# New instruction lists, loads and PSUM banks for an attention block, and a last batch that ends in two parts

## The chip, the cores and the metric

The kernel runs on one core of one Trainium2 chip. The metric is the device time of one execution in microseconds (us), lower is better; the number compared is the median of several executions. The profile is one execution taken by the hardware profiler: it shows when each instruction ran on each engine. The engines are PE (TensorE: matrix multiplications into PSUM), ACT (ScalarE), DVE (VectorE), POOL (GpSimd) and SP (SyncE, which here only issues transfers); PEld is PE's weight load, which overlaps the multiplications. Each engine has its own instruction list and runs it in order; they meet through semaphores.

## The reference

```python
B, Sq, D = 8, 112, 640
H, Sk, Dh = 32, 512, 192
...
q = (lambda x, *d: x.transpose(*d))((x @ wq).reshape(B, Sq, H, Dh), 0, 2, 1, 3)
scores = jnp.einsum("bhqd,bhkd->bhqk", q, k_cache) * (Dh ** -0.5)
p = _softmax(scores, axis=-1)
o = jnp.einsum("bhqk,bhkd->bhqd", p, v_cache)
return (lambda x, *d: x.transpose(*d))(o, 0, 2, 1, 3).reshape(B, Sq, H * Dh) @ wo
```

Inputs and output are bf16. The K and V caches are the bulk of the bytes read: 8 x 32 heads of 512 x 192 each.

## The kernel before

The heads are worked off in four rounds of eight (`NR`, `HU`). A round has the eight batches, and a batch in a round has two steps of four heads (`qd`), so there are 64 steps n (`NN`); n // 2 numbers the K and V blocks. A group g (`NG` = 8) is half a round: four batches, for which the queries and the output product are made together.

What a step needs is made by named operations, and these names stand in the lists:

- `('XT', c)` transposes a piece of x on PE, `evX` copies it out of PSUM.
- `('Q', g, lp, c)` (line 721) is one 128-column piece of the query product for a group: five matmuls of 448 columns; `evQ` copies it out. `('qc', n)` makes a copy shifted by half the partitions, on POOL mostly.
- `('KT', i, p)` (line 673) transposes K on PE for those blocks that were loaded as they lie (`PLAIN`: blocks 0 to 5 and 14; transfer `KN`), 24 transposes of 64 rows each; `evK` copies them out, in two halves. The other blocks come transposed by the transfer itself (`K`, line 158).
- `('Sm', n, j)` and `('St', n, j)` (line 774) are the scores of two heads: `Sm` is the first 128 of the 192 contraction rows, the full array; `St` the remaining 64, two row tiles of 64 side by side.
- `smax`, `exp`, `rc`, `norm` (lines 831, 836, 848, 840) are the softmax: minimum of the negated scores and copy to SBUF on DVE, exponential with its sum on ACT, reciprocal and scaling on DVE.
- `('PT', n)` (line 875) transposes the probabilities: 32 small transposes, row tiles of 64 and 48; `evPT` copies them out, part 0 with 768 and part 1 with 1024 columns. Steps 57 to 61 (`BY_DMA`) are transposed by a transfer instead (`TD`, line 859).
- `('PVt', n)` and `('PVm', n, j)` (lines 907 and 919) are probabilities times values. `PVm` makes 128 of the 192 output rows of each head with the full array, `PVt` (the "value rests") the other 64 of two heads side by side: 16 matmuls with column tiles of 64. `evPV` copies both out.
- `('O', g, m, part)` (line 941) is the output product of a group for one block m of 128 output columns, in two halves of six matmuls; `oacc` adds it to a running sum in `accT` on DVE. For the last group the third batch is done by `O6` (line 974) and the fourth, the last batch of all, by `OL` (line 998); `oacc6` and `oaccL` (lines 1007 and 1011) add these. `OF` (line 1023) transposes a batch of the result back, `oout` copies it to SBUF and the transfer `OUT` (line 646) writes it.

On PE the operations are of three kinds, by how the array is divided: the full array (XT, Q, Sm, PVm, O, O6, OL, OF), rows in two (KT, St, PT) and columns in two (PVt).

Nothing orders itself at run time. `ORDER_PE`, `ORDER_ACT`, `ORDER_DVE`, `ORDER_POOL` and `ORDER_SP` (lines 236 to 574) are written out by hand or by a planner beforehand, and each engine runs its list. `Plan.run` puts a wait ahead of an operation for each semaphore count that its inputs need. `copy` (line 144) takes the engine in whose list a copy stands. `BANKS` (line 575) gives each PSUM tile its bank; a tile waits until the copy of the bank's previous holder is done (`holder`). SP's transfers go out in list order; each waits until its place is free (`k_place_free`, `pv_all`, `q_done`) and, by `AHEAD`, until enough of the earlier ones have landed:

```python
        for i, op in enumerate(ORDER_SP):
            behind = [k for k in range(i) if sum(map(size, ORDER_SP[k + 1:i])) >= AHEAD]
            if behind and op[0] != "OUT":
                P.ops[op]["deps"] = P.ops[op]["deps"] + [ORDER_SP[behind[-1]]]
```

## Time and profile before

| | |
|---|---|
| median of 3 runs | 436.23 us (436.13 to 437.5) |
| the profiled execution's own time | 434.56 us |
| its span, first to last instruction | 432.8 us |
| PE busy | 418.6 us, 97%, 6805 matmuls |
| DVE busy | 345.8 us, 80%, 1087 instructions |
| ACT busy | 335.9 us, 78%, 734 instructions |
| POOL busy | 88.7 us, 20% |
| bytes moved by transfers | 122.05 MB, mean 282 GB/s |

The busy time of an engine is the time in which at least one of its instructions runs. A row of the timeline has the start in us from the beginning of the span, the time until the last of the merged instructions ends, the engine and line, the operation with its output and inputs, the shape (for PE the rows x columns of the array, then the operand), the number of instructions merged, and in brackets the idle time before with what ended it. Matmuls are pipelined, so that the time from one start to the next says what a matmul costs the list, and its own duration does not. A row of the waits has who waited for whom: us in total, times, longest.

### The profile page before, as it was taken

The page shows a single profiled execution, that of the slowest core. Times are in us where ns is not written, and L with a number is a line of the kernel's source. Part 1 is how long each engine was busy: PE and PEld are TensorE (multiplying, and loading weights), DVE is VectorE, ACT ScalarE, POOL GpSimd, SP SyncE. Part 2 cuts the span into 40 slices and gives each one's busy share as a digit, 9 for nine tenths or more (in the row PEclk, how much of TensorE's full clock was granted, in tenths as well). Part 3 has the DMA queues.
Part 4 walks back from the last instruction along what each step waited for, and adds up shares of the span by engine and source line. Part 5 has one row for each costly group of instructions (what it writes and reads, how often), then busy time and mean ns, then how long its engine had stood idle before and what let it go on. Part 6 is the DMA issues. An engine that isn't in the chain of part 4 may idle for free.

```text
span 432.8 us, 16330 instructions
## 1 busy us (share of the span) xinstructions
PE 418.6 (97%) x6805; PEld 289.6 (67%) x6805; DVE 345.8 (80%) x1087; ACT 335.9 (78%) x734; POOL 88.7 (20%) x124
## 2 busy tenths in 40 slices
PE   6999997999999999999999999999999999999996
PEld 4566665666767666677767656776667666666786
DVE  1689878889778888888798897869888688988871
ACT  3489988988868686979877957988778877776774
POOL 0102121222212221322122122212222120212100
PEclk9999999999999999999999999999999999999999
DMA  7999999999999999999999999999999999999872
GB/s 254 371 337 334 335 309 238 326 355 179 229 343 257 220 334 374 341 230 343 290 222 335 299 222 324 368 359 214 244 259 268 211 282 368 312 241 247 207 216 84
DMA packets 218923, 122.05 MB, mean 282 GB/s; under 512 B 165216, under 2 KB 218848, under 8 KB 218848
## 3 DMA queue, kind: packets, MB, share of 16 engines
q1 hardware_dynamic: 218848, 120.99, 107.6%
q8 instruction: 54, 0.88, 0.8%
q14 instruction: 21, 0.17, 0.1%
HBM read 78.22 MB, written 1.15 MB: 183 GB/s over the span
## 4 chain that ended last, share of the span: by engine, by line
PE 86%; DMA 6%; DVE 4%; ACT 1%; issue 1%; SPq 0%; DVEq 0%; ACTq 0%
PE ps L721 19%; PE ps L774 19%; PE ps L941 18%; PE ps L919 12%; PE ps L907 7%; PE ps L875 7%; PE ps L673 2%; DVE s_sb L831 2%; DMA wq_sb<-in_wq_dram 2%; DMA vt<-in_v_cache_dram 2%; DMA wq_sb<-p_sb 1%; DMA accT<-in_k_cache_dram 1%; DVE p_sb L840 1%; PE ps L974 1%; ACT p_sb L836 1%
## 5 line engine op out<-in xcount | busy, mean ns | idle before, releaser
L836 ACT ACTIVATE p_sb<-s_sb,nmx 112x512 bf16<-112x512 f32 x256 | 182.6, 716 | 34.4 <-DVE s_sb L831 28.6
L831 DVE TENSOR_SCALAR_CACHE_REDUCE s_sb<-ps 112x512 f32<-112x512 f32 x256 | 169.5, 683 | 30.1 <-PE ps L774 22.1
L762 POOL COPY qh<-qr 64x672 bf16<-64x672 bf16 x59 | 44.0, 746 | 309.8 <-PE ps L774 266.7
L721 PE MATMUL ps<-xT_sb,wq_sb 128*128 128x448 bf16 x480 | 101.7, 353 | 4.2 <-DMA wq_sb<-in_wq_dram 2.7
L774 PE MATMUL ps<-kt,qr 128*128 128x256 bf16 (+1 forms) x512 | 95.3, 272 | 0.2
L941 PE MATMUL ps<-oT_sb,wo_sb 128*128 128x448 bf16 (+1 forms) x480 | 91.4, 341 | 0.0
L840 DVE TENSOR_SCALAR p_sb<-p_sb,rinv 112x512 bf16<-112x512 bf16 x256 | 88.3, 374 | 0.8
L774 PE MATMUL ps<-kt,qh 128*128 128x256 bf16 (+1 forms) x512 | 87.7, 272 | 0.0
L721 PEld LDWEIGHTS ps<-xT_sb,wq_sb 128*128 128x128 bf16 x480 | 42.6, 98 | 41.0 <-DMA wq_sb<-in_wq_dram 3.7
L941 PEld LDWEIGHTS ps<-oT_sb,wo_sb 128*128 128x128 bf16 x480 | 44.8, 98 | 36.0 <-issue 0.4
L146 ACT ACTIVATE oT_sb<-ps 128x672 bf16<-128x672 f32 x64 | 46.3, 724 | 24.8 <-PE ps L919 24.4
L146 ACT ACTIVATE pT_sb<-ps 128x1024 bf16<-128x1024 bf16 (+1 forms) x61 | 55.8, 921 | 10.9 <-PE ps L875 10.9
L774 PEld LDWEIGHTS ps<-kt,qr 128*128 128x128 bf16 (+1 forms) x512 | 44.1, 96 | 21.4 <-issue 12.9
L919 PE MATMUL ps<-pT_sb,vt 128*128 128x112 bf16 x944 | 55.3, 213 | 0.0
L919 PEld LDWEIGHTS ps<-pT_sb,vt 128*128 128x128 bf16 x944 | 47.5, 98 | 4.0
L836 ACT ACTIVATION_READ_ACCUMULATOR p_sb<-s_sb,nmx 112x1 f32 x256 | 49.1, 192 | 0.0
L774 PEld LDWEIGHTS ps<-kt,qh 128*128 128x128 bf16 (+1 forms) x512 | 44.1, 96 | 6.0
L763 POOL COPY qh<-qr 64x672 bf16<-64x672 bf16 x59 | 44.0, 745 | 2.5
L146 ACT ACTIVATE qr<-ps 128x448 bf16<-128x448 f32 x58 | 31.0, 538 | 14.6 <-PE ps L721 14.4
L147 DVE COPY pT_sb<-ps 128x768 bf16<-128x768 bf16 (+1 forms) x57 | 34.6, 608 | 7.9 <-PE ps L875 7.7
L875 PE MATMUL ps<-ident,p_sb 64*128 64x64 bf16 (+1 forms) x1888 | 37.3, 185 | 1.8 <-issue 1.2
L875 PEld LDWEIGHTS ps<-ident,p_sb 64*128 64x128 bf16 (+1 forms) x1888 | 33.5, 94 | 7.6 <-issue 3.5
(58 smaller groups left out, 268.7 us busy)
## 6 DMA issues: line engine op xcount, KB each, us to landing
vt<-in_v_cache_dram SPq DMA_DIRECT2D x64, 768.0 KB, 6.8
wo_sb<-in_wo_dram SPq DMA_DIRECT2D x8, 960.0 KB, 7.5
wq_sb<-in_wq_dram SPq DMA_DIRECT2D x7, 960.0 KB, 7.3
wo_sb<-in_k_cache_dram SPq DMA_DIRECT2D x6, 768.0 KB, 7.5
accT<-in_k_cache_dram SPq DMA_DIRECT2D x4, 768.0 KB, 6.1
vt<-in_k_cache_dram SPq DMA_DIRECT2D x2, 768.0 KB, 8.5
kt<-in_k_cache_dram SPq DMA_DIRECT2D x2, 768.0 KB, 6.9
out_dram<-xT_sb SPq DMA_DIRECT2D x8, 140.0 KB, 2.3
```

What stands on the lines that cost most here:

```text
L146: return e.activation(dst, src, ACTF.Copy)
L147: return e.tensor_copy(dst, src)
L721: mm = e.matmul(ps[:, bank, 0:SG], w, v, start=(dc == 0), stop=(dc == DC - 1))
L762: e.tensor_copy(dst[64:128, :, 0:3, :], src[0:64])
L763: return e.tensor_copy(dst[0:64, :, 1:4, :], src[64:128])
L774: return e.matmul(ps[:, 2 * j + odd, hs], q, ktb[j][lo:hi, :, blk, h * 128:(h + 1) * 128], start=first, stop=last, skip_group_check=True)
L831: return e.tensor_scalar(s_sb[:, a, :].rearrange("p (e c) -> p e c", e=2), ps[0:SQ, 2 * j:2 * j + 2, h * 256:(h + 1) * 256], -scale, None, ...
L836: return e.activation(p_sb[:, k, :], s_sb[:, a, :], ACTF.Exp, bias=nmx[:, k:k + 1], scale=-1.0, accum_out=rsum[:, k:k + 1])
L840: return e.tensor_scalar(p_sb[:, k, :], p_sb[:, k, :], rinv[:, k:k + 1], None, op0=ALU.mult)
L875: ends.append(e.transpose(psb[:, bank + t, i * w:(i + 1) * w], p_sb[lo:hi, (4 * n + k) % 8, q * 128:(q + 1) * 128], ident[lo:hi, lo:hi]))
L919: mm = e.matmul(ps[:, b0 + j, 2 * h * SQ:(2 * h + 1) * SQ], vtb[:, h0 + 2 * j + h, d0:d0 + 128], pT(j, h, q), start=(q == 0), stop=(q == 3))
L941: mm = e.matmul(ps[:, bank_of["O", g, m], 0:nc_], wo_sb[:, k, m * 128:(m + 1) * 128], oT_sb[:, g % 2, k, 0:nc_], start=(k == 0), stop=(k = ...
```

## The change

All five engine lists but POOL's, the order of loads and the table of banks are replaced. The same operations are done, but for the last batch. What the new lists do differently, as far as it can be said in words:

- PE: neighbours of different kinds number 238 and not 249; in 19 places and not 10 a `PVt` stands directly behind a `PT`. Early on some `KT` and `Q` are exchanged, and `KT` of block 2 comes together.
- ACT and DVE: 10 of the `evK` and 10 of the larger `evPT` copies go from ACT to DVE, 2 `evX` and 1 `evQ` from DVE to ACT.
- SP: V 2 is loaded later and V 0 earlier among the first pieces; later blocks are exchanged; at the end V 31 goes ahead of OUT 2 and OUT 1.
- Banks: other numbers; `XT` 0 and `XT` 1 now share bank 4.

The last batch (7) ends in two parts: `OL` and `oaccL` go by the blocks 0 to 2 and 3 to 4 (`ENDS`, in place of 0, 1, 4 and 2, 3), so that each `oaccL` is one addition; `OF` and `oout` of batch 7 are split in the same way, with a bank each; the transfer waits for both copies. The second copy and that of batch 6 are in DVE's list.

```diff
--- before.py
+++ after.py
         ORDER_PE = [
...
-            ('KT', 0, 0), ('KT', 0, 1), ('Q', 0, 1, 2), ('XT', 4), ('Q', 0, 0, 2), ('Q', 0, 3, 0), ('XT', 5),
-            ('Q', 0, 2, 1), ('Sm', 0, 0), ('Sm', 0, 1), ('St', 0, 0), ('St', 0, 1), ('KT', 0, 3), ('Q', 0, 3, 1),
-            ('Q', 0, 3, 2), ('KT', 0, 2), ('KT', 1, 2), ('KT', 1, 1), ('Q', 0, 2, 0), ('XT', 6), ('Q', 0, 2, 2),
-            ('Q', 1, 0, 1), ('KT', 2, 1), ('KT', 1, 3), ('Sm', 1, 0), ('Sm', 1, 1), ('St', 1, 0), ('St', 1, 1),
-            ('Q', 1, 1, 0), ('KT', 1, 0), ('KT', 2, 3), ('KT', 2, 2), ('Q', 1, 0, 0), ('Q', 1, 0, 2), ('Q', 1, 1, 1),
-            ('Sm', 2, 0), ('Sm', 2, 1), ('KT', 2, 0), ('St', 2, 0), ('St', 2, 1), ('PT', 0), ('Q', 1, 2, 0), ('Q', 1, 3, 2),
...
-            ('Q', 2, 0, 2), ('PT', 5), ('PVt', 4), ('KT', 5, 3), ('PVm', 4, 0), ('PVm', 4, 1), ('Sm', 8, 0), ('Sm', 8, 1),
...
-            ('PVt', 62), ('PVt', 63), ('PVm', 62, 0), ('PVm', 62, 1), ('PVm', 63, 0), ('PVm', 63, 1), ('OF', 5),
-            ('OL', 0, 1), ('OL', 0, 0), ('OL', 1, 0), ('OL', 1, 1), ('OF', 6), ('OF', 7)]
+            ('KT', 0, 0), ('KT', 0, 1), ('Q', 0, 1, 2), ('XT', 4), ('XT', 5), ('Q', 0, 0, 2), ('Q', 0, 3, 0),
+            ('Q', 0, 2, 1), ('Sm', 0, 0), ('Sm', 0, 1), ('KT', 0, 3), ('KT', 0, 2), ('St', 0, 0), ('St', 0, 1),
+            ('Q', 0, 2, 0), ('Q', 0, 3, 2), ('XT', 6), ('Q', 0, 2, 2), ('KT', 1, 1), ('Q', 0, 3, 1), ('Q', 1, 0, 1),
+            ('KT', 1, 2), ('KT', 1, 3), ('KT', 2, 1), ('Sm', 1, 0), ('Sm', 1, 1), ('St', 1, 0), ('St', 1, 1),
+            ('Q', 1, 1, 0), ('Q', 1, 0, 0), ('KT', 1, 0), ('KT', 2, 3), ('KT', 2, 2), ('KT', 2, 0), ('Q', 1, 1, 1),
+            ('Sm', 2, 0), ('Sm', 2, 1), ('St', 2, 0), ('St', 2, 1), ('PT', 0), ('Q', 1, 0, 2), ('Q', 1, 2, 1),
...
+            ('Q', 2, 0, 2), ('Q', 2, 1, 2), ('KT', 5, 3), ('PT', 5), ('PVt', 4), ('PVm', 4, 0), ('PVm', 4, 1),
...
+            ('O', 7, 3, 1), ('PVt', 61), ('PVm', 61, 0), ('PVm', 61, 1), ('O6', 1, 0), ('PT', 62), ('O6', 1, 1), ('OF', 1),
+            ('O6', 0, 0), ('O6', 2, 0), ('OF', 3), ('O6', 0, 1), ('O6', 2, 1), ('PT', 63), ('PVt', 62), ('PVm', 62, 0),
+            ('PVm', 62, 1), ('PVt', 63), ('PVm', 63, 0), ('PVm', 63, 1), ('OL', 0, 0), ('OF', 5), ('OF', 4), ('OL', 1, 0),
+            ('OL', 0, 1), ('OL', 1, 1), ('OF', 6), ('OF', 7, 0), ('OF', 7, 1)]
         ORDER_ACT = [
...
-            ('evPT', 63, 1), ('oout', 4), ('evPV', 62), ('evPV', 63), ('oout', 5), ('oout', 6), ('oout', 7)]
...
+            ('evPT', 62, 1), ('oout', 3), ('evPV', 62), ('evPV', 63), ('oout', 5), ('oout', 4), ('oout', 7, 0)]
         ORDER_DVE = [
...
-            ('norm', 63, 3), ('evPT', 62, 0), ('oacc6', 2), ('evPT', 63, 0), ('oacc6', 1), ('oaccL', 0), ('oaccL', 1)]
...
+            ('norm', 63, 1), ('evPT', 63, 1), ('evPT', 63, 0), ('oacc6', 1), ('oacc6', 0), ('oacc6', 2), ('oaccL', 0),
+            ('oaccL', 1), ('oout', 6), ('oout', 7, 1)]
         ORDER_SP = [
...
-            ('KN', 0, 4, 4), ('KN', 1, 0, 4), ('KN', 1, 4, 4), ('V', 2, 0), ('KN', 2, 0, 4), ('V', 2, 1), ('KN', 2, 4, 4),
-            ('V', 0, 0), ('V', 0, 1), ('KN', 3, 4, 4), ('KN', 4, 4, 4), ('KN', 3, 0, 4), ('KN', 4, 0, 4), ('V', 1, 1),
...
-            ('K', 30), ('K', 31), ('TD', 57), ('TD', 58), ('V', 29, 0), ('V', 29, 1), ('TD', 59), ('TD', 60), ('V', 30, 1),
-            ('V', 30, 0), ('TD', 61), ('OUT', 2), ('OUT', 1), ('V', 31, 0), ('V', 31, 1), ('OUT', 4), ('OUT', 0),
-            ('OUT', 3), ('OUT', 5), ('OUT', 6), ('OUT', 7)]
...
+            ('KN', 0, 4, 4), ('KN', 1, 0, 4), ('KN', 1, 4, 4), ('KN', 2, 0, 4), ('V', 0, 0), ('KN', 2, 4, 4), ('V', 2, 0),
+            ('KN', 3, 4, 4), ('V', 0, 1), ('V', 1, 1), ('KN', 3, 0, 4), ('V', 1, 0), ('KN', 4, 4, 4), ('KN', 4, 0, 4),
...
+            ('K', 30), ('V', 26, 1), ('V', 27, 1), ('V', 26, 0), ('WO', 3, 0), ('V', 27, 0), ('WO', 3, 1), ('V', 28, 0),
+            ('V', 28, 1), ('K', 31), ('TD', 57), ('TD', 58), ('V', 29, 0), ('V', 29, 1), ('TD', 59), ('TD', 60),
+            ('V', 30, 1), ('V', 30, 0), ('TD', 61), ('V', 31, 0), ('OUT', 0), ('V', 31, 1), ('OUT', 2), ('OUT', 1),
+            ('OUT', 5), ('OUT', 3), ('OUT', 4), ('OUT', 6), ('OUT', 7)]
         BANKS = [
...
-            (('XT', 0), 5), (('XT', 1), 4), (('XT', 3), 7), (('XT', 2), 6), (('Q', 0, 1, 1), 7), (('Q', 0, 0, 0), 5),
...
+            (('XT', 0), 4), (('XT', 1), 4), (('XT', 3), 5), (('XT', 2), 6), (('Q', 0, 1, 1), 7), (('Q', 0, 0, 0), 5),
...
+            (('OF', 6), 2), (('OF', 7, 0), 5), (('OF', 7, 1), 0)]
         for kind, *a in ORDER_SP:
...
         for b in range(B):
             def emit(e, b=b):
                 return e.dma_start(out[b], xT_sb[0:SQ, b % DC, 0:D])
-            add("SP", ("OUT", b), [("oout", b)], emit, f"mOUT{b % DC}", 16)
+            add("SP", ("OUT", b), [("oout", b)] if b < B - 1 else [("oout", b, 0), ("oout", b, 1)], emit, f"mOUT{b % DC}", 16)
...
-        LAST = {0: (7, 0), 1: (7, 1), 4: (7, 2), 2: (6, 0), 3: (6, 1)}
+        LAST = {0: (7, 0), 1: (7, 1), 2: (7, 2), 3: (6, 0), 4: (6, 1)}
+        ENDS = [(0, 1, 2), (3, 4)]
 
         def o_last(s, part):
-
-            blocks = (0, 1, 4) if part == 0 else (2, 3)
 
             def emit(e):
                 for k in range(6 * s, 6 * s + 6):
                     w, o = wo_k(k, 3)
-                    for m in blocks:
+                    for m in ENDS[part]:
                         bank, c = LAST[m]
                         mm = e.matmul(ps[:, bank, c * SQ:(c + 1) * SQ], w[:, m * 128:(m + 1) * 128], o,
                                       start=(k == 0 and c == 0), stop=(k == KB - 1), skip_group_check=True)
@@ -1002,34 +1002,31 @@
 
         def o_last_acc(part):
             def emit(e):
-                bank = 7 - part
-                m0 = 2 * part
-                mm = e.tensor_tensor(oF[:, 1, m0:m0 + 2, 3 * SQ:SG, 0],
-                                     ps[:, bank, 0:2 * SQ].rearrange("p (c s) -> p c s", c=2),
-                                     accT[:, 1, m0:m0 + 2, 3 * SQ:SG], op=ALU.add)
-                if part == 0:
-                    mm = e.tensor_tensor(oF[:, 1, 4, 3 * SQ:SG, 0], ps[:, bank, 2 * SQ:3 * SQ], accT[:, 1, 4, 3 * SQ:SG],
-                                         op=ALU.add)
-                return mm
+                m0, n = ENDS[part][0], len(ENDS[part])
+                return e.tensor_tensor(oF[:, 1, m0:m0 + n, 3 * SQ:SG, 0],
+                                       ps[:, 7 - part, 0:n * SQ].rearrange("p (c s) -> p c s", c=n),
+                                       accT[:, 1, m0:m0 + n, 3 * SQ:SG], op=ALU.add)
             add("DVE", ("oaccL", part), [("OL", 1, part)] + [("oacc", NG - 3, m) for m in range(DC)], emit)
 
 
-        def o_final(b):
+        def o_final(b, *part):
             bh, bb = divmod(b, B // 2)
-            bank = bank_of["OF", b]
-
-            def emit(e):
-                for m in range(DC):
+            bank = bank_of["OF", b, *part]
+            blocks = ENDS[part[0]] if part else tuple(range(DC))
+            cols = slice(blocks[0] * 128, blocks[-1] * 128 + 128)
+
+            def emit(e):
+                for m in blocks:
                     mm = e.transpose(psb[0:SQ, bank, m * 128:(m + 1) * 128], oF[:, bh, m, bb * SQ:(bb + 1) * SQ, 0],
                                      ident[:, :])
                 return mm
 
             def evac(e):
-                return copy(("oout", b), e, xT_sb[0:SQ, b % DC, 0:D], psb[0:SQ, bank, 0:D])
-            need = ([("oaccL", 0), ("oaccL", 1)] if b == B - 1 else [("oacc6", g) for g in range(3)] if b == B - 2 else
+                return copy(("oout", b, *part), e, xT_sb[0:SQ, b % DC, cols], psb[0:SQ, bank, cols])
+            need = ([("oaccL", *part)] if part else [("oacc6", g) for g in range(3)] if b == B - 2 else
                     [("oacc", NG - 2 + bh, m) for m in range(DC)])
-            add("PE", ("OF", b), need, emit)
-            add("ACT", ("oout", b), [("OF", b), *wq_last] + ([("OUT", b - DC)] if b >= DC else []), evac)
+            add("PE", ("OF", b, *part), need, emit)
+            add("ACT", ("oout", b, *part), [("OF", b, *part), *wq_last] + ([("OUT", b - DC)] if b >= DC else []), evac)
 
 
         for c in range(B * SQ // 128):
@@ -1067,8 +1064,10 @@
             o_last(s, 1)
         o_last_acc(0)
         o_last_acc(1)
-        for b in range(B):
+        for b in range(B - 1):
             o_final(b)
+        o_final(B - 1, 0)
+        o_final(B - 1, 1)
```

463 lines of the change are left out of this document (234 added, 229 removed), and 265 rows, old and new, of tables (BANKS, ORDER_PE, ORDER_POOL, ORDER_SP).

## The prediction

> **What bounds the kernel now.** I read the head of the page first, with the chain that ended last, then the list of waits, then single stretches of the timeline.
>
> ```profile
> span 432.8 us, 16330 instructions
> PE 418.6 (97%) x6805; PEld 289.6 (67%) x6805; DVE 345.8 (80%) x1087; ACT 335.9 (78%) x734; POOL 88.7 (20%) x124
> PE 86%; DMA 6%; DVE 4%; ACT 1%; issue 1%; SPq 0%; DVEq 0%; ACTq 0%
> ...
> PE ps L721 <- DMA wq_sb<-in_wq_dram: 2.7, 2, 2.3
> PE ps L721 <- DVE kt L147: 1.6, 1, 1.6
> PE ps L875 <- issue: 1.2, 2, 0.6
> PE ps L907 <- DMA wq_sb<-p_sb: 0.7, 1, 0.7
> PE ps L974 <- issue: 0.6, 1, 0.6
> PE ps L907 <- issue: 0.6, 1, 0.6
> ...
> PE ps L907 <- ACT pT_sb L146: 0.3, 1, 0.3
> ```
>
> TensorE is busy for 97% of the span and carries 86% of the chain. Its waits are few and short, and the longest is the first weight load. So the end is set by how long PE's list takes to issue, plus these waits. An edit earns something only if it makes that list shorter or removes one of these waits.
>
> **The changes of tiling.** In the lists I sort PE's operations into three kinds: full array (XT, Q, Sm, PVm, O, O6, OL, OF), row-tiled (KT, St, PT: 64 rows) and column-tiled (PVt: 64 columns). Walking down `ORDER_PE`, neighbours of different kinds number 249 in the old list and 238 in the new one, so the change does what it says. Value rests straight behind PT go from 10 to 19. Behind full-array work (Q, O, Sm, PVm, OF) they fall from 30 to 24. From row-tiled to full-array work there is one change anyway; a PVt put in between makes it two, so it adds one, where a PVt amid full-array work adds two. That is where most of the eleven go. What one change costs is read from starts in the timeline of PE:
>
> ```profile
> 160.48 0.63 PE L875 MATMUL ps<-ident,p_sb 64*128 64x64 bf16 x32
> 161.04 1.12 PE L721 MATMUL ps<-xT_sb,wq_sb 128*128 128x448 bf16 x5
> ...
> 225.28 2.43 PE L941 MATMUL ps<-oT_sb,wo_sb 128*128 128x448 bf16 x12
> 227.55 0.27 PE L774 MATMUL ps<-kt,qr 128*128 128x256 bf16 x1
> ...
> 241.21 2.44 PE L941 MATMUL ps<-oT_sb,wo_sb 128*128 128x448 bf16 x12
> 243.58 0.98 PE L907 MATMUL ps<-pT_sb,vt 128*64 128x112 bf16 x32
> 244.49 1.70 PE L919 MATMUL ps<-pT_sb,vt 128*128 128x112 bf16 x31
> ...
> 300.57 0.58 PE L907 MATMUL ps<-pT_sb,vt 128*64 128x112 bf16 x16
> 301.09 0.96 PE L919 MATMUL ps<-pT_sb,vt 128*128 128x112 bf16 x16
> ```
>
> Twelve output matmuls take 2.27 us (225.28 to 227.55) with full-array work behind them, and 2.37 us (241.21 to 243.58) with column-tiled work behind them, so entering costs 0.10. Sixteen rests take 0.52 us and thirty-two take 0.91 before the full-array mains, so leaving costs 2 x 0.52 - 0.91 = 0.13. I take 0.10, because the first pair is the longer and cleaner one: 11 x 0.10 = 1.1 us off PE's list, with 1.1 and 1.4 as bounds. Nothing hides a change, as PE has no other work at that moment. All else on PE is the same number of matmuls in another order.
>
> [...]
>
> **The early loads.** Two waits in the first 32 us hang on K pieces:
>
> ```profile
> 21.72 0.52 PE L673 MATMUL ps<-ident,vt 64*128 64x64 bf16 x24
> 22.69 0.87 PE L673 MATMUL ps<-ident,wo_sb 64*128 64x64 bf16 x48 [0.45 <-DMA wo_sb<-in_k_cache_dram]
> 23.50 0.74 PE L721 MATMUL ps<-xT_sb,wq_sb 128*128 128x448 bf16 x3
> ...
> 30.18 0.53 PE L673 MATMUL ps<-ident,wo_sb 64*128 64x64 bf16 x24
> 30.95 0.87 PE L673 MATMUL ps<-ident,accT 64*128 64x64 bf16 x48 [0.25 <-DMA accT<-in_k_cache_dram]
> ...
> 22.72 0.37 SPq L167 DMA_DIRECT2D vt<-in_v_cache_dram  x1
> 24.68 0.37 SPq L189 DMA_DIRECT2D accT<-in_k_cache_dram  x1
> ```
>
> Forty-eight transposes and one change take 0.81 us (22.69 to 23.50), so 24 take 0.36. The starts at 21.72 and 22.69 are 0.97 apart: 0.6 us was waited. 30.18 to 30.95 is 0.77: 0.4 us. The first is ('KT', 1, 2). The new list puts five operations ahead of it (three Q of five matmuls at 2.27/12 = 0.19, one XT and one KT: more than 3 us), while its load keeps its place in SP's queue, so the wait goes. The second is ('KT', 2, 3). Its load now has one V half ahead of it where it had two; SP issued the neighbours 22.72 and 24.68, 2 us apart, so it lands about 2 us sooner and the 0.4 goes too. What is later for it is V 2, which the rests of step 4 are the first to read, far down the list. I take -1.0 us; the bounds are -1.2 (a further short wait on a Q) and 0, if PE waits for the softmax instead. Both X pieces that now share bank 4, ('XT', 0) and ('XT', 1), cost PE one copy of 0.7 to 0.8 us between them; it lies under the wait on wq (2.3 us, above), and would be 0.8 us if that load came sooner. Later loads are reordered at equal bytes. V 31 no longer stands behind OUT 2 and OUT 1 in SP's queue (its second half behind OUT 0 alone), which is room, not time; V 26 and V 27 now stand behind K 30, and what waits for them is the rests of steps 52 and 54.
>
> **Where PE's code comes from.** Four waits of PE end on "issue" (1.2, 0.6 and 0.6 us above), and the one put down to "DVE kt" follows a copy long done. I counted instructions at each:
>
> ```profile
> q8 instruction: 54, 0.88, 0.8%
> ...
> 0.00:48.40 48.40, 43.34 (x725) 28.35 (x726) 32.22 (x95) 32.73 (x67) 6.63 (x14) 1.00 0.96 326
> 0.00:61.85 61.85, 56.14 (x977) 36.68 (x978) 44.50 (x134) 45.78 (x95) 9.60 (x18) 1.00 0.98 325
> 0.00:68.60 68.60, 61.34 (x1103) 40.52 (x1104) 49.09 (x148) 51.46 (x106) 10.51 (x20) 1.00 1.00 316
> ```
>
> Matmuls and weight loads together stand at 1451, 1955 and 2207 there: 504 and 252 apart. That is a fixed grain, and 54 packets of 16 KB over PE's 13,610 matmuls and loads make 252 each. So these are late code blocks: 1.2 + 1.6 + 0.6 + 0.6 = 4.0 us in all. They come where 252 instructions pass quickly, that is where transposes and rests crowd. Adding durations like those above along the lists, the six blocks from 34 us of work on last 4.15 to 6.8 us in the old list and 4.8 to 6.3 in the new one, so the crowding is more even and no less in sum. At the last of the waits, among the O6, the blocks are alike (4.73 and 4.75), but V 31 is issued earlier and leaves the queues idle. I take -0.6, one wait of the five. The bounds are -4.0 and, with two more of the largest (1.6), +3.2.
>
> **Copies that change engines.** Ten K copies and ten PT copies move from ACT to DVE:
>
> ```profile
> L146 ACT ACTIVATE pT_sb<-ps 128x1024 bf16<-128x1024 bf16 x35 | 35.4, 1014 | 6.3 <-PE ps L875 6.3
> L147 DVE COPY pT_sb<-ps 128x1024 bf16<-128x1024 bf16 x24 | 16.4, 685 | 4.0 <-PE ps L875 3.8
> L147 DVE COPY kt<-ps 128x768 bf16<-128x768 bf16 x29 | 15.7, 552 | 2.4 <-PE ps L673 2.3
> ...
> 20.00:60.00 40.00, 38.38 (x789) 25.70 (x787) 35.56 (x111) 37.48 (x82) 8.58 (x12) 1.00 1.00 342
> ```
>
> DVE gains 10 x 0.685 + 10 x 0.552 = 12.4 us, ACT loses more, since a PT copy lasts 1.014 there. Over the whole span that leaves DVE near 83%. Between 20 and 60 us it is busy 35.56 of 40 and gets seven of the K copies, 3.9 us, so 99%. Behind each copy stand the maxima and norms that the next PT needs. Five PTs also have their rests nearer: 1.35 to 1.5 us of PE work behind them, where the nearest old one had 1.0 and waited 0.3. I take +0.5; the bounds are 0 and 3.9 + 5 x 0.3 = 5.4.
>
> **The end in two parts.**
>
> ```profile
> 428.37 0.41 DVE L1007 TENSOR_TENSOR accT<-ps,accT 128x224 bf16<-128x224 f32 x1
> 428.65 1.41 ACT L146 ACTIVATE xT_sb<-ps 112x640 bf16<-112x640 bf16 x2 [1.33 <-PE ps L1023]
> 428.83 0.49 PE L1023 MATMUL ps<-ident,accT 128*112 128x128 bf16 x5 [0.22 <-DVE accT L1007]
> ...
> L147 DVE COPY xT_sb<-ps 128x640 bf16<-128x640 bf16 x5 | 2.4, 487 | 6.8 <-PE ps L656 6.8
> ```
>
> Behind the last addition (428.78) come five transposes and a copy of 0.70, to 430.06. The new end has three transposes and their copy done beforehand; behind the same addition DVE makes the copy of batch 6 (0.49), then 256 columns of batch 7 (0.30 by the step from 640 to 768 columns, 0.487 to 0.552), while the two transposes pass underneath. That ends at 429.6. SP must issue OUT 6 just before, which took it 0.3 to 0.4 us for a plain transfer above. I take -0.4, with bounds 0 and -0.7.
>
> **The sum** is -1.1 - 1.0 - 0.6 + 0.5 - 0.4 = -2.6 us. The profiled execution took 434.56, so 432.0. The median of the runs shown is 436.23, 1.67 above that execution; the same step gives 433.6, which is my forecast.
>
> **Rivals.** First, *the waits only move*: PE runs ahead of the softmax early on and waits for it, so the loads and the code give nothing; -1.1 - 0.4 + 0.9 (three of the five near PTs at 0.3) = -0.6, thus 435.6. For it speaks ACT and DVE at 37.48 and 35.56 of 40; against it, that of PE's waits only 0.3 us is put down to ACT's PT copies.
>
> Second, *DVE becomes the bound between 20 and 60 us* and this is slower: the loads' gain goes and PE waits for all seven K copies, 3.9 us: -1.1 - 0.6 + 3.9 = +2.2, thus 438.4. It decides once the added work passes DVE's free 4.4 us there. Against it: ACT gives up more than DVE takes, and both feed the same chain.
>
> Third, *the code comes in time*: all 4.0 us go, not 0.6: 430.2.
>
> **Chances.** Forecast 0.50, waits only move 0.22, DVE bound 0.14, code in time 0.14. A measurement here tells 0.3% (1.3 us) from no change, so faster is below 434.9: 0.64; same 0.22; slower 0.14. The range 430.3 to 437.8 leaves out most of the slower rival and the outer half of the code's bounds; the likeliest case alone has 432.3 to 434.9.
>
> **What would show it.** Right: PE's starts after tiling changes still 0.10 apart from the plain ones; the two K waits gone before 32 us; the last copy ending 0.8 us behind the last addition, not 1.3; PE's waits on DVE between 20 and 60 us below 1 us. Wrong: new PE waits on "DVE s_sb", "DVE p_sb" or "pT_sb" of over 2 us in sum, a PE wait on V, or code waits summing to more than 5 us.

## The result and the profile after

The kernel with the change takes 447.77 us (median of 444.28, 446.67, 448.87 and 449.78), the kernel before 436.18 beside it. The ratio is 1.027, with a 95% interval of 1.022 to 1.033: slower by 11.6 us, where 2.6 us faster was forecast. The profiled execution took 444.28, 9.7 more than the profiled one of before, and it is the quickest of the four; the traces below explain this part. Some executions of a kernel take over 1.5% longer than its fastest, mostly at a lower granted clock (0.985 to 0.992; one at 1.0); medians, ratios and intervals below leave them out.

First the head of the page, the chain's shares and the row of TensorE's granted clock (40 slices, tenths) of the kernel after.

```profile
span 442.1 us, 16292 instructions
PE 422.2 (96%) x6805; PEld 289.7 (66%) x6805; DVE 356.9 (81%) x1105; ACT 322.4 (73%) x716; POOL 88.9 (20%) x124
...
PEclk8999999999999999999999999999999999999999
...
PE 85%; DVE 6%; issue 3%; DMA 3%; ACT 2%; SPq 0%; DVEq 0%; ACTq 0%
```

The span grew by 9.3 us. PE works 3.6 us longer (422.2 against 418.6) on the same 6,805 matmuls, and its share of the chain hardly moved; "issue" went from 1% to 3%. The first digit of the clock row is 8, where before's is 9. Next the list of PE's waits in the kernel after: what PE waited for, us in total, times, longest.

```profile
PE ps L674 <- issue: 2.1, 1, 2.1
PE ps L722 <- issue: 1.9, 2, 1.0
PE ps L876 <- DVE p_sb L841: 1.4, 2, 1.2
PE ps L908 <- DMA wq_sb<-p_sb: 1.3, 1, 1.3
PE ps L920 <- issue: 1.1, 2, 0.7
...
PE ps L722 <- DMA wq_sb<-in_wq_dram: 1.1, 1, 1.1
PE ps L876 <- issue: 1.0, 1, 1.0
PE ps L657 <- ACT xT_sb L146: 0.8, 1, 0.8
```

Over the whole list, waits by what ended them: DMA 4.1 us before and 2.4 after, DVE 3.1 and 4.2, ACT 0.3 and 1.8, issue 2.4 and 7.5; together 9.9 and 15.9. PE's idle time in all (span less busy time) grew by 5.7 us, from 14.2 to 19.9; with the 3.6 us of longer work this is the 9.3. No DMA row is left at L674, the K transposes: the two waits on K pieces went, as forecast. Three other things came.

**The code blocks.** Timeline of PE in the kernel after (start, us, instructions; in brackets the idle time ahead):

```profile
74.75 0.44 PE L674 MATMUL ps<-ident,wo_sb 64*128 64x64 bf16 x18
77.25 0.26 PE L674 MATMUL ps<-ident,wo_sb 64*128 64x64 bf16 x6 [2.07 <-issue]
...
82.81 0.86 PE L920 MATMUL ps<-pT_sb,vt 128*128 128x112 bf16 x14
84.12 0.26 PE L920 MATMUL ps<-pT_sb,vt 128*128 128x112 bf16 x2 [0.46 <-issue]
```

PE stops in the middle of a list entry, 18 transposes into 24, with everything there but its own instructions. The windows from 0 to these points count them:

```profile
0.00:77.20 77.20, 69.90 (x1232) 45.02 (x1232) 56.80 (x169) 54.30 (x114) 11.09 (x20) 0.98 0.98 313
0.00:84.10 84.10, 76.31 (x1358) 49.52 (x1359) 63.24 (x191) 60.28 (x127) 13.00 (x23) 0.98 1.00 307
```

2464 and 2717 matmuls and loads: 253 apart, where it was 252 before. Counted from one start to the next at all boundaries, with the usual step taken off, such waits sum to 4.9 us before, five of them, and 9.15 after, nine of them, the longest 2.3. (The idle times of the list alone make 4.0 and 7.5 for the same waits.) In the trace of the queues, packets that carry PE's code start 0.4 to 7.3 us after the boundary is passed, and PE goes on 2.2 to 2.7 us after its packet started. At 77.25 the start came over 6 us late, and SP's queue shows what was on its way:

```profile
68.14 19.86 SPq L158 DMA_TRANSPOSE kt<-in_k_cache_dram  x3
```

The first of these three transposing K transfers was issued 0.2 us ahead of the boundary, at 68.4. The packet started at 74.66, half a microsecond after SP had finished issuing it (74.14).

This is the case for five of the nine late blocks, 5.5 us of the waits: SP was issuing a transposing transfer when their boundary was passed. For the other four (at 49, 199, 387 and 422 us, 3.5 us) it was not. Over this whole trace 21 boundaries are passed during such an issue; 15 of the fetches start within 1.5 us of its end and six sooner.

**The clock.** PE's start in the kernel after, then 4 us of windows (after the comma PE, PEld, DVE, ACT and POOL busy with counts, then the granted clock) after and, below, before:

```profile
6.25 1.01 PE L657 MATMUL ps<-ident,kt 128*128 128x128 bf16 x15 [0.80 <-ACT xT_sb L146]
8.34 5.62 PE L722 MATMUL ps<-xT_sb,wq_sb 128*128 128x448 bf16 x20 [1.07 <-DMA wq_sb<-in_wq_dram]
13.90 0.88 PE L674 MATMUL ps<-ident,vt 64*128 64x64 bf16 x48
```

```profile
8.00:12.00 4.00, 3.66 (x11) 1.55 (x12) 0.19 (x1) 0.54 (x1) 0.00 (x0) 0.57 1.04 375
```

```profile
8.00:12.00 4.00, 3.54 (x18) 1.70 (x19) 0.94 (x2) 0.54 (x1) 0.00 (x0) 1.00 1.06 384
```

The clock fell to 0.57 of full speed for this stretch, and 11 query matmuls fit where 18 did. The clock record of the trace has 0.50 for 3.41 us, from 8.54 to 11.96. That is 1.7 us of work lost, nearly half of the 3.6 us that PE works longer.

**DVE's order and the loads.** PT 10 waits 1.2 us for the scaling of its own probabilities. And the loads fall behind; a window of before, then of after, with the mean GB/s at the end of the row:

```profile
0.00:372.00 372.00, 362.91 (x5879) 245.62 (x5881) 303.17 (x949) 295.02 (x646) 81.15 (x114) 1.00 1.12 294
```

```profile
0.00:372.00 372.00, 358.18 (x5821) 241.44 (x5822) 304.79 (x941) 280.03 (x620) 79.83 (x112) 1.00 1.09 284
```

At 372 us the kernel before has moved 109.4 MB (294 x 372) and the one after 105.6, some 13 us of its mean rate less, while PE's busy time is 4.7 us lower (358.18 against 362.91).

### The profile page after: what moved, and what is told of

It is laid out like the page before. It is cut to its first block, busy times and chain, and to the rows that moved or that the text cites. A ratio compares the mean times of both kernels' runs of the same rounds, so it can differ in the third digit from the quotient of the medians.

```text
span 442.1 us, 16292 instructions
## 1 busy us (share of the span) xinstructions
PE 422.2 (96%) x6805; PEld 289.7 (66%) x6805; DVE 356.9 (81%) x1105; ACT 322.4 (73%) x716; POOL 88.9 (20%) x124
## 3 DMA queue, kind: packets, MB, share of 16 engines
HBM read 78.22 MB, written 1.15 MB: 180 GB/s over the span
## 4 chain that ended last, share of the span: by engine, by line
PE 85%; DVE 6%; issue 3%; DMA 3%; ACT 2%; SPq 0%; DVEq 0%; ACTq 0%
PE ps L722 20%; PE ps L775 19%; PE ps L942 17%; PE ps L920 12%; PE ps L908 7%; PE ps L876 7%; DVE s_sb L832 3%; PE ps L674 2%; DVE p_sb L841 2%; DMA wq_sb<-in_wq_dram 1%; ACT p_sb L837 1%; DMA wq_sb<-p_sb 1%; PE ps L975 1%; PE ps L998 1%; PE ps L1020 1%
## 5 line engine op out<-in xcount | busy, mean ns | idle before, releaser
L942 PE MATMUL ps<-oT_sb,wo_sb 128*128 128x448 bf16 (+1 forms) x480 | 92.4, 341 | 0.0
L841 DVE TENSOR_SCALAR p_sb<-p_sb,rinv 112x512 bf16<-112x512 bf16 x256 | 90.7, 386 | 0.6
L722 PEld LDWEIGHTS ps<-xT_sb,wq_sb 128*128 128x128 bf16 x480 | 43.6, 99 | 43.8 <-issue 5.0
L920 PE MATMUL ps<-pT_sb,vt 128*128 128x112 bf16 x944 | 56.2, 213 | 1.1 <-issue 1.1
L146 ACT ACTIVATE pT_sb<-ps 128x768 bf16<-128x768 bf16 (+1 forms) x51 | 45.6, 902 | 11.9 <-PE ps L876 11.7
L147 DVE COPY pT_sb<-ps 128x768 bf16<-128x768 bf16 (+1 forms) x67 | 40.7, 619 | 6.6 <-PE ps L876 6.3
L876 PE MATMUL ps<-ident,p_sb 48*128 48x48 bf16 (+1 forms) x1888 | 37.5, 185 | 2.8 <-DVE p_sb L841 1.4
```

What stands on the lines that cost most here:

```text
L146: return e.activation(dst, src, ACTF.Copy)
L147: return e.tensor_copy(dst, src)
L722: mm = e.matmul(ps[:, bank, 0:SG], w, v, start=(dc == 0), stop=(dc == DC - 1))
L841: return e.tensor_scalar(p_sb[:, k, :], p_sb[:, k, :], rinv[:, k:k + 1], None, op0=ALU.mult)
L876: ends.append(e.transpose(psb[:, bank + t, i * w:(i + 1) * w], p_sb[lo:hi, (4 * n + k) % 8, q * 128:(q + 1) * 128], ident[lo:hi, lo:hi]))
L920: mm = e.matmul(ps[:, b0 + j, 2 * h * SQ:(2 * h + 1) * SQ], vtb[:, h0 + 2 * j + h, d0:d0 + 128], pT(j, h, q), start=(q == 0), stop=(q == 3))
```

## The experiments

The theory from these traces was: late code blocks (about 4 us), the first bank with the clock that it costs (about 2 us), and the order on DVE (some 2 us). The rivals were the copies that changed engines, the tiling, and the loads.

**The first bank.**

```diff
-            (('XT', 0), 4), (('XT', 1), 4), (('XT', 3), 5),
+            (('XT', 0), 7), (('XT', 1), 4), (('XT', 3), 5),
```

> The changed kernel with one number of the bank table altered: the first X transposes get bank 7, so that the second need not wait for the first one's copy (0.96 us in the changed kernel's trace). Theory START (that wait leaves TensorE cold when the first weights land: the first ten query matmuls take 0.5 and 0.7 us more than before): the wait and the cold matmuls go, 1.0 to 1.3 us faster than the changed kernel (447.8), so about 446.6. Theory CODE (the loss is late code blocks) and theory CHAIN (it is the softmax's copies on VectorE): the weights land at 8.3 us all the same, the wait on them grows from 1.1 to 2.1 us, and the time stays within 0.5 us of 447.8.

Measured: 444.36, 445.01 and 446.79 us, ratio 1.022 (1.015 to 1.029). Its start, timeline of PE:

```profile
7.58 1.10 PE L722 MATMUL ps<-xT_sb,wq_sb 128*128 128x448 bf16 x5 [1.07 <-DVE xT_sb L147]
9.01 3.01 PE L722 MATMUL ps<-xT_sb,wq_sb 128*128 128x448 bf16 x15 [0.33 <-DMA wq_sb<-in_wq_dram]
11.96 0.87 PE L674 MATMUL ps<-ident,vt 64*128 64x64 bf16 x48
```

The first K transposes start at 11.96 where they started at 13.90: one bank number costs 1.9 us, 0.8 by the later start of the queries (8.34 against 7.58) and the rest by the slow clock. Against the kernel before, where they start at 12.52, it is 1.4 us. The slow clock need not come with the bank: of the traces kept, both with the shared bank have it at 8 us, and so has one of the 13 without it (that of "More changes of tiling" below, from 8.3 us on, behind one wait of 2.03 us). The span did not fall (442.9), because another drop came at 76 to 80 us, behind the same code wait, in the window of this kernel:

```profile
76.00:80.00 4.00, 4.00 (x54) 2.17 (x47) 3.83 (x12) 3.44 (x8) 0.00 (x0) 0.66 1.27 290
```

**The copies back.** All 125 copies that changed engines stand on before's engines again (71 from DVE to ACT, 54 the other way), placed by the trace's times.

```diff
 ORDER_DVE:  -('evK', 1, 0, 1)  -('evK', 1, 1, 1) ...  +('evK', 0, 3, 1)  +('evK', 1, 2, 1) ...
 ORDER_ACT:  the other way round
```

> The changed kernel with every copy out of PSUM (K, PT, query, X) on the engine that had it before, 125 copies exchanged between ScalarE and VectorE, each put into its new engine's list at the place that its start in the trace gives it. Lists of TensorE, loads and banks stay as changed. Theory CHAIN: TensorE's waits on VectorE that are new (1.28 us before PT 10, 0.58 before the scores of step 21, 0.4 before PT 50 and others, some 3 us) go: 444.5 to 445.5. Theory CODE: the late code blocks (9.15 us in the changed kernel against 4.87) stay, and the time stays within 1.5 us of 447.8; it may be slower, as the copies' places were not chosen for these engines.

Measured: 455.23 us, ratio 1.045 (1.038 to 1.051), 7.5 us slower than the change itself; PE's waits on DVE rose from 4.2 to 8.1 and on ACT from 1.8 to 7.3. So putting the copies back alone does not bring the loss back; the new placing fits the new lists better. The run cannot tell how well before's placing would do in lists planned for it.

**The grain of the code alone.** The kernel before, with 64 tiny matmuls (16 columns, into a bank nobody reads) under the first wait on wq, so that every later code boundary lies 128 instructions further up the list.

```diff
+        def pad(e):
+            for i in range(64):
+                mm = e.matmul(ps[0:16, 3, 0:16], zeros[:, 0:16], zeros[:, 0:16], start=True, stop=True)
+            return mm
```

> The kernel before with 64 tiny matmuls (16 columns by 16 columns, result unused) put into TensorE's wait for the first query weights, which lasts 2.3 us; nothing else is altered. It moves every later boundary of a code block by 128 instructions. Theory CODE: the late blocks come at other places; with the time from one boundary to the next worked out from the trace of before, and the delays of the fetches as they were at those times, their sum grows from 4.9 to about 8.5 us: 439 to 440.5. If code blocks have no such part in the time: 436.2, at most 0.5 more if the 64 matmuls outlast the wait.

Measured: 442.28 us, ratio 1.014 (1.008 to 1.019). The first K transposes start 0.16 us later than before (12.68 against 12.52), so the added matmuls themselves cost next to nothing. The waits of PE:

```profile
PE ps L675 <- issue: 2.9, 2, 1.8
PE ps L877 <- issue: 2.0, 1, 2.0
```

Code waits by count of instructions went from 4.9 to 7.9 us, and behind two of them, at 33 and 70 us, came 3.4 us at half the clock. So the same operations in the same order lose 5.9 us by where the boundaries fall (1.0135 x 436.37).

**The end alone.** The kernel before, with OL, its additions and the last transposes and copy in two parts (the code of the change, its lists at the end alone).

```diff
-            ('OL', 1, 1), ('OF', 6), ('OF', 7)]
+            ('OL', 1, 1), ('OF', 6), ('OF', 7, 0), ('OF', 7, 1)]
```

> The kernel before with the end in two parts alone: OL, oaccL, OF and oout of the last batch split as in the change, the copy of batch 6 and the second copy of batch 7 at the end of VectorE's list, all other lists, loads and banks as before. By the prediction's step: 0.4 us faster (435.8), with bounds 0 and 0.7. Rival: the issue of the transfer of batch 6 or the second copy's wait stands in the way and nothing is gained (436.2).

Measured: 435.18 us (median of eight), ratio 0.998 (0.995 to 1.001); the span is that of before, 432.8. The end of the kernel after, timeline of all engines, and then of before's SP:

```profile
437.79 0.41 DVE L1006 TENSOR_TENSOR accT<-ps,accT 128x224 bf16<-128x224 f32 x1 [0.64 <-PE ps L998]
438.10 0.81 DVE L147 COPY xT_sb<-ps 112x640 bf16<-112x640 bf16 x2
...
438.61 1.18 SPq L647 DMA_DIRECT2D out_dram<-xT_sb  x2
```

```profile
429.38 1.02 SPq L646 DMA_DIRECT2D out_dram<-xT_sb  x2
```

The last copy ends 0.71 us behind the last addition (438.91 against 438.20) where it ended 1.28 behind before. But the last transfer goes out 1.22 us behind the addition (439.42), against 1.30 before (430.08): issuing OUT 6, right ahead, holds SP for 0.7 us. Of the copy's 0.57 us about 0.1 reaches the transfer in this trace. That is no fixed price: in nine other traces with this end the issue takes 0.32 to 0.53 us and the last transfer goes out 0.82 to 1.43 us behind the addition (1.15 in this experiment's, with an issue of 0.32), so that between nothing and 0.5 us is won.

**Without most of the K transfers at 68 to 88 us.** The kernel with the first bank mended, with the transfers of K 6, 7 and 8 bringing one head in eight (the rest of those K blocks is left out).

```diff
+                if i in (6, 7, 8):
+                    src, dst = src[0:128], dst[:, :, 0:128]
```

> The kernel of the run x1_first_bank (445.9) in which the three transfers K 7, K 6 and K 8, which come back to back from 66 us on, bring only one head in eight; the rest of their places keeps older data, so the scores of these blocks are not the reference's, but every engine has the same instructions. Theory CODE (code blocks are late because their fetch queues behind the transfers already issued, and a K transfer of 6 us is the longest): the fetches of the blocks reached at about 74, 83 and 90 us start within 4 us of the boundary and not 4.5 to 6.2; the waits there (2.1 + 1.2 us and what the cold clock adds behind the first, some 1 to 1.5) go: 441 to 442.5. Theory CHAIN: the waits at these places have to do with VectorE's order and stay; within 1 us of 445.9.

Measured: 442.4 us, ratio 1.016 (1.010 to 1.022). PE's waits:

```profile
PE ps L911 <- DMA wq_sb<-p_sb: 2.0, 2, 1.1
PE ps L725 <- DMA wq_sb<-in_wq_dram: 1.7, 2, 1.3
PE ps L677 <- issue: 1.6, 1, 1.6
...
PE ps L911 <- DMA vt<-in_v_cache_dram: 1.1, 2, 0.7
```

The code waits at 74, 83 and 90 us are gone, and their sum is 4.96 us where it was 9.85 in the kernel that this one differs from. So the K transfers are what delays the code there. Of the 4.9 us, 2.6 reached the span (442.9 to 440.3, and the ratio went from 1.022 to 1.016); PE's waits on DMA rose from 1.1 to 5.4, of which 3.1 are for V and for the transposed probabilities, late in the list. The row of 1.6 us on "issue" is a late block at 62 us, ahead of all the K transfers: its fetch started 5.3 us after the boundary with none on its way.

**The order on DVE.** The kernel with the first bank mended, and four exchanges in DVE's list, of which the first is:

```diff
-            ('smax', 12, 0), ('rc', 11, 0), ('rc', 10, 0), ('norm', 11, 1), ('norm', 10, 2), ('rc', 11, 1), ('norm', 11, 0), ('norm', 10, 1), ('norm', 10, 0),
+            ('rc', 10, 0), ('norm', 10, 2), ('norm', 10, 1), ('norm', 10, 0), ('smax', 12, 0), ('rc', 11, 0), ('norm', 11, 1), ('rc', 11, 1), ('norm', 11, 0),
```

> The kernel of the run x1_first_bank with four exchanges in VectorE's list: what PE waited for goes ahead of what it waited behind (the reciprocal and three scalings of step 10 ahead of the first maximum of step 12; the second maximum of step 20 ahead of a scaling of 19; the same in step 52; the last scaling of step 42 ahead of two other operations). Theory CHAIN: the waits of 1.28, 0.58, 0.34 and 0.40 us in front of PT 10, the scores of step 21, PT 42 and PT 50 go or fall to a third, and the time falls by 1.5 to 2.3 us to about 444. Rival: the order only decides who waits; each gain is used up at the next late operation (or late code block) and the time stays within 0.7 us of 445.9.

Measured: 444.85 us, ratio 1.024 (1.016 to 1.031), where it was 1.022 without the exchanges: no gain that can be told. PE's waits on DVE fell from 5.6 to 2.2, and on DMA they rose from 1.1 to 6.5. Timeline of PE near the end:

```profile
379.87 0.58 PE L911 MATMUL ps<-pT_sb,vt 128*64 128x112 bf16 x16 [2.52 <-DMA vt<-in_v_cache_dram]
```

The wait at 379.87 is for V 26, which stands behind K 30 in SP's list; K 30's place comes free with the scores of step 53. What PE gains earlier ends here.

**V 26 ahead of K 30.** The kernel of the last experiment, with K 30 moved behind V 28.

```diff
-            ('K', 30), ('V', 26, 1), ('V', 27, 1), ('V', 26, 0), ('WO', 3, 0), ('V', 27, 0), ('WO', 3, 1), ('V', 28, 0), ('V', 28, 1), ('K', 31),
+            ('V', 26, 1), ('V', 27, 1), ('V', 26, 0), ('WO', 3, 0), ('V', 27, 0), ('WO', 3, 1), ('V', 28, 0), ('V', 28, 1), ('K', 30), ('K', 31),
```

> The kernel of the run x8_norms_first (444.85) with one transfer moved: K 30 goes out behind V 28 and ahead of K 31, as in the kernel before, and not ahead of V 26 and V 27. K 30 has to wait for a place that the scores of step 53 set free, and V 26, V 27 and the wo pieces queue behind it on SyncE. Theory LOADS (what the early gains win is lost at PVt 52, which waits 2.52 us for V 26, and at the steps behind it): that wait goes, V 26 lands some 5 us sooner, and the time falls by 1.5 to 3 us to 442 to 443.3. Rival: the next late transfer (the transposed probabilities of steps 57 and 59, 1.16 and 1.34 us in the run before) takes up the gain; within 0.7 us of 444.85.

Measured: 439.46 us in the profiled execution (span 437.3, clock 0.999), and 446.76, 448.39 and 450.45 in the others, whose mean clock was 0.987 to 0.992. The gain rests on one execution, so no ratio is given and it is not secured. In it the wait on V 26 is gone and the span is 4.6 us shorter than in the last experiment; the next wait of this kind is for the transposed probabilities of TD 57:

```profile
396.17 0.58 PE L912 MATMUL ps<-wq_sb,vt 128*64 128x112 bf16 x16 [1.08 <-DMA wq_sb<-p_sb]
```

**The grain in the new lists.** The same kernel with 24 tiny matmuls under the first wait, so 48 instructions further.

```diff
+            for i in range(24):
+                mm = e.matmul(ps[0:16, 3, 0:16], zeros[:, 0:16], zeros[:, 0:16], start=True, stop=True)
```

> The kernel of the run x11_v26_first with 24 tiny matmuls (16 by 16) in TensorE's wait for the first query weights, nothing else: every boundary of a code block comes 48 instructions, some 1.2 us, earlier. In the kernels with the new lists the boundary at 67 us falls 0.2 us behind the issue of K 7 and its fetch starts 6.2 to 6.6 us later. Theory CODE: it now falls ahead of K 7, the fetch starts 2 to 4 us later, and the wait of 2.3 us at 74 to 76 us goes: 1.5 to 2.5 us faster than the run beside it (x11_v26_first), if the other boundaries lose nothing. Rival: other boundaries become as late as this one was: within 1 us of it.

Measured: 447.59 us, ratio 1.027 (1.023 to 1.032), clock 0.987 in the profiled execution. The boundary moved as intended, to 0.9 us ahead of K 7's issue (66.56 against 67.47), and the fetch started 7.2 us after it all the same, when that issue was over (73.51). PE's timeline:

```profile
73.12 0.27 PE L782 MATMUL ps<-kt,qh 128*128 128x256 bf16 x1
76.34 0.40 PE L782 MATMUL ps<-kt,qh 128*128 128x256 bf16 x1 [2.95 <-issue]
```

This is the longest code wait of all, and behind it the clock is low, 0.50 from 76 to 80 us: one score matmul takes 0.40 us, not 0.27. This shift of the grain does not mend it. Near the end the wait for the transposed probabilities has grown too, in the row of PE's waits:

```profile
PE ps L915 <- DMA wq_sb<-p_sb: 4.1, 2, 3.6
```

**All four mended at once.** The kernel with V 26 ahead, with the short K transfers 6, 7 and 8 (seven heads in eight of these left out).

```diff
+                if i in (6, 7, 8):
+                    src, dst = src[0:128], dst[:, :, 0:128]
```

> The kernel of the run x11_v26_first (bank of the first X piece, four exchanges on VectorE, V 26 ahead of K 30) in which K 7, K 6 and K 8 bring only one head in eight, as in the run x7_short_k; the scores of these blocks are not the reference's. It takes away all four causes named for the new lists' loss. If they are all of it: the late code blocks at 75 to 90 us (4.3 us of the profiled execution of x11_v26_first, 439.5) go and with them the drop of TensorE's clock that came behind the wait of 2.3 us in the slower executions (446.8 to 450.5): 434.5 to 437, and all executions within 3 us. If something else costs the new lists as much: over 440, or still a spread of 10 us.

Measured: 443.26, 443.53 and 445.98 us, ratio 1.019 (1.016 to 1.022). This is some 7 us above the kernel before (436.31), so these four causes are not the whole of the loss, or the gains do not add up. No trace of these three executions is kept, so what PE waited for in them stays open. Nor do the runs show that the clock fell behind the wait of 2.3 us in the executions of 446.8 to 450.5 us: of these they give the mean clock alone, 0.987 to 0.992.

**More changes of tiling.** The kernel before, with 50 steps' scores in the order Sm, St, Sm, St: 349 changes, not 249.

```diff
-            ('Sm', 0, 0), ('Sm', 0, 1), ('St', 0, 0), ('St', 0, 1),
+            ('Sm', 0, 0), ('St', 0, 0), ('Sm', 0, 1), ('St', 0, 1),
```

> The kernel before with the scores in another order: in the 50 steps where the two full-array parts and the two row-tiled parts stand together (full, full, rows, rows), they go full, rows, full, rows. That makes 349 changes of tiling out of 249 and alters nothing else. By the prediction's price of 0.10 us a change: 10 us slower, 446 to 447. If a change costs nothing of its own (the price was read from pairs that differ in something else): within 1 us of 436.3. If more was hidden than the pairs show: over 449.

Measured: 443.03 us, ratio 1.020 (1.013 to 1.027). The busy row of its page:

```profile
PE 429.0 (97%) x6805; PEld 283.2 (64%) x6805; DVE 345.6 (78%) x1087; ACT 336.3 (76%) x734; POOL 89.2 (20%) x124
```

PE works 10.4 us longer for 100 changes: 0.104 us each, where 0.10 was read from the starts. (1.7 of it is a stretch at half the clock, from 8.3 to 11.7 us; but the starts say the same: the 16 score matmuls of a step take 1.42 us before and 1.63 here, medians of the 50 steps, 0.106 for each of two changes.) The median rose by 7.1 us, as PE's waits fell by 2.1.

**K transfers in a row in the kernel before.** Before's loads in an order like the new one: both halves of V 4, WQ, then K 7, K 6 and K 8 in a row.

```diff
-            ('KN', 5, 0, 4), ('K', 6), ('WQ', 1, 2, 2), ('K', 7), ('V', 4, 1), ('V', 5, 0), ('V', 4, 0), ('WO', 0, 1),
+            ('KN', 5, 0, 4), ('V', 4, 0), ('WQ', 1, 2, 2), ('V', 4, 1), ('K', 7), ('K', 6), ('K', 8), ('V', 5, 0), ('WO', 0, 1),
```

> The kernel before with the loads between the last piece of K 5 and K 10 in another order, so that K 7, K 6 and K 8 go out in a row, as in the change, with both halves of V 4 ahead of them; all else as before. Theory CODE: the boundaries of code blocks at 62 to 90 us now find the queue filled by transposing transfers; their fetches start 5 to 6 us after the boundary and not 2 to 5, the late blocks of that stretch cost 4 to 6 us and not 3.3, with a cold clock behind a wait of over 2 us: 437.5 to 440. Rival: the loads' order has no part in it: within 0.7 us of 436.3.

Measured: 444.04 us, ratio 1.020 (1.014 to 1.026), but not by the code: code waits fell to 2.1 us. Timeline of PE:

```profile
104.35 5.60 PE L942 MATMUL ps<-oT_sb,wo_sb 128*128 128x448 bf16 x18 [7.72 <-DMA wo_sb<-in_wo_dram]
```

The output weights stand behind the three K transfers and come 7.7 us late. So theory CODE was wrong on this order. Three boundaries are passed while these K transfers are issued (72, 79 and 85 us), the fetch starts 3.1 to 3.8 us later, not 5 to 6, and no block waits over 0.1 us: K transfers in a row do not by themselves make the code late. And WO 0 has no slack.

**The end with loads of its own.** So the next one is before with the end in two parts, K 7 and K 6 together, K 8 left behind K 9, and both WO 0 ahead of V 6.

```diff
-  ('K', 6), ('WQ', 1, 2, 2), ('K', 7), ('V', 4, 1), ('V', 5, 0), ('V', 4, 0), ('WO', 0, 1), ('V', 6, 0), ('V', 5, 1), ('WO', 0, 0), ('V', 6, 1),
+  ('V', 4, 0), ('WQ', 1, 2, 2), ('V', 4, 1), ('K', 7), ('K', 6), ('V', 5, 0), ('WO', 0, 1), ('WO', 0, 0), ('V', 6, 0), ('V', 5, 1), ('V', 6, 1),
```

> The kernel of the run x5_end_only (435.5) with the loads between the last piece of K 5 and K 10 in another order: both halves of V 4 ahead of K 7 and K 6, then V 5's first half and both wo pieces, then V 6 and V 5, K 9, K 8. It is the order of the run x10_k_in_a_row, in which no code block came late between 40 and 100 us, with K 8 put back so that the wo pieces land in time (7.7 us were waited for them there). Theory CODE: the late blocks at 62, 69 (0.6 and 1.6 us, another 0.8 at 75 in some traces) fall away and no load wait comes: 432.5 to 434.5. Rival: late blocks come back elsewhere, as the boundaries now meet other transfers: within 1 us of 435.5.

Measured: 433.58 us over 12 executions against 436.14 for the kernel before, ratio 0.9945 (0.991 to 0.998): faster than both kernels. PE's waits:

```profile
PE ps L737 <- DMA wq_sb<-in_wq_dram: 1.9, 2, 1.5
PE ps L790 <- DVE s_sb L847: 1.5, 1, 1.5
```

Code waits went from 4.9 to 1.8 us, with 0.9 off the span of the profiled execution; the rest turned into waits on DVE's maxima. Of the 0.9, 0.4 us is won up to the last addition (428.40, where it was 428.77) and 0.5 behind it, by the end in two parts.

**The two early K waits alone.** The last kernel, with V 2 behind the K pieces of block 2 and ('KT', 1, 2) two operations later.

```diff
-            ('KT', 1, 2), ('KT', 1, 1), ('Q', 0, 2, 0), ('XT', 6),
+            ('KT', 1, 1), ('Q', 0, 2, 0), ('KT', 1, 2), ('XT', 6),
```

> The kernel of the run x12_end_and_loads (433.6) with the second step of the prediction alone: V 2 is loaded behind the K pieces of block 2, and ('KT', 1, 2) stands two operations later, so that TensorE's two waits for K pieces before 32 us (0.7 and 0.7 us in that run) go. By the prediction's term of 1.0 us: 432 to 433. Rival: the gain does not reach the end, since TensorE then waits for the softmax or a late code block instead: 433 to 434.5.

Measured: 434.62 us, ratio 0.996 (0.994 to 0.998), the same span as without (431.9). PE's waits on DMA fell from 3.3 to 1.9 us, on issue they rose from 0.8 to 2.2. The waits go, and the end does not come sooner.

## Why the prediction was wrong, point by point

- **Tiling, -1.1 us: right as a price, partial as a gain.** A change costs 0.104 us in the experiment, so eleven are worth 1.1. But only 7 of 10 us of such work reached the end there, and no run takes the new PE order alone.
- **The early loads, -1.0: the mechanism was right, the end was not reached.** Both waits went. With them alone gone the span stayed (431.9), the bound of 0 that the step named. A wait taken out at 30 us is worth something only if no wait behind it takes it over.
- **The shared bank: costed at nothing, 1.9 us (1.4 against the kernel before).** The step read the start as covered by the wait on wq, "0.8 us if that load came sooner". The load did come sooner: PE waits 1.07 us on it, not 2.3, in a list that also had 0.8 of idle ahead. What the step did not price is the clock: two short idle times in a row, 0.80 and 1.07 us, were followed by half the clock for 3.4 us. That this follows the bank each time is not shown.
- **The code blocks, -0.6 with bounds -4.0 and +3.2: the step that failed.** It is +4.3 us, 4.9 to 9.15, outside the bounds. The one wait that the step took away, among the O6, did go. But the step took the wait only from how fast 252 instructions pass; the traces show that it hangs as much on when the fetch starts, 0.4 to 7.3 us after the boundary. The block at 77.25 had 6.8 us of work ahead of it, above the 4.8 to 6.3 of the step, and still came 2.3 us late, as its fetch started 6.3 us after the boundary, behind a K transfer. Cutting three of these transfers short took 4.9 us of code waits away. The place of the K transfers, called "reordered at equal bytes", is thus a part of the price that the step left out; it is not all of it, as four of the nine late blocks met none.
- **Copies that change engines, +0.5: right in its place.** Between 20 and 60 us PE's longest wait on DVE is 0.47, below the 1 us named; the rival of a bound DVE did not come. Ten and ten copies are only the net: 125 changed engines. Elsewhere DVE's order cost 2.3 us (1.21 at PT 10, 0.60 ahead of the scores of step 21, 0.33 and 0.18 at two later PT), which no step had looked at.
- **The end, -0.4: right for the copy, unsure for the transfer.** The copy ends 0.57 us nearer to the addition, but in the profiled execution SP's issue of OUT 6, taken at 0.3 to 0.4, lasted 0.7, and 0.1 us is left; in other runs with this end the issue is as the step took it and up to 0.5 is left.
- **"V 26 and V 27 now stand behind K 30": named without a price.** It cost nothing in the kernel after, where no wait of PE is on V, and 2.52 us in "The order on DVE", where PE came there earlier.
- **The rivals.** None of the three happened. The slower side was placed in DVE; it lay mostly in the code that came late, with a smaller part in DVE's order outside that stretch. Two marks said wrong: code waits of more than 5 us, and new waits on "DVE s_sb" and "DVE p_sb" of over 2 us in sum (2.8 in the list above, 0.2 before).

The code, the start of PE and DVE's order sum to 4.3 + 1.4 + 2.3 = 8.0 of the 9.3 us of the span, with nothing taken off for the gains in tiling and early loads, so that some of the loss has no name. And the runs in which these three were taken away did not return that much; in two of them PE then met later loads. **Open** are four things: why some fetches behind a K transfer start after about 1 us (0.6 to 1.4) and others after 6 to 7; what delays the fetches that meet no K transfer; what decides whether a wait of about 2 us is followed by a low clock; and what still parts the best execution of the mended new lists (439.46) from the kernel before.

## What to carry to other kernels

Where PE waits on "issue" in the middle of an entry, count its instructions from the start of the span: here a fixed spacing of 252 led to the code, whose packets started up to 7.3 us after the boundary. The longest of these waits went when the long transfers beside their boundaries were cut short or placed elsewhere, so the order of loads is the first thing to try. Price an early stall with the clock that follows it, not only with its own length: here 1.7 us of work was lost behind 0.80 and 1.07 us of idle. In lists where every load has its place by what it waits for, a gain ahead of a load is only real if that load can come sooner too: follow each moved load to the place that it waits for before calling it room.

## What the runs showed of the hardware

**A scaling on DVE takes nearly twice as long beside a copy on POOL (619 ns, not 346).** Timeline of the kernel after, DVE and then POOL:

```profile
98.75 0.35 DVE L841 TENSOR_SCALAR p_sb<-p_sb,rinv 112x512 bf16<-112x512 bf16 x1
...
102.32 1.85 DVE L841 TENSOR_SCALAR p_sb<-p_sb,rinv 112x512 bf16<-112x512 bf16 x3
```

```profile
102.23 0.74 POOL L763 COPY qh<-qr 64x672 bf16<-64x672 bf16 x1
103.02 0.74 POOL L764 COPY qh<-qr 64x672 bf16<-64x672 bf16 x1
```

Alone it takes 0.35 us, and three in a row, two of them beside the copies, take 1.85. Over the kernel, the 41 that overlap a copy have a median of 619 ns, the other 215 one of 346; before, 31 have 602 and 225 have 347. Three such slow ones stand between the maxima and PT 10, which waits 1.2 us. The price is thus some 0.27 us for a meeting at the median (619 - 346) and up to 0.56 (the longest takes 907 ns). POOL's copies take the same either way: 743 ns at the median beside a scaling, 742 without. What holds the scaling up, no trace shows.

**Half the clock came behind some waits of about 2 us, and behind others none.** Each drop ahead of the last microseconds of a kernel is half the clock for 3.4 us or twice that in these traces (3.41 in the kernel after); a mean of 0.57 or 0.66 over 4 us is such a stretch. At the start of the kernel after, 0.80 and 1.07 us of idle were followed by one; a code wait of 1.9 us (first bank mended, at 75.8 us) was followed by one, and one of 2.07 us in the kernel after by none. A wait on wq of 2.03 us was followed by one (more changes of tiling), and those of 2.3 and 2.5 us in the kernel before and in "The end alone" by none. So the length of these waits does not tell whether the clock falls, and what decides it, no run shows.
